# The first eight weight pieces may be scheduled freely, and batch 0's second query part is written ahead of the main loop

## The chip, the cores and the metric

The kernel runs on one core of a Trainium2 chip. The metric is the device time of one execution in microseconds (us); the median of three runs before the change is 893.13 us (891.83 to 895.79). The profile and the trace come from one further, profiled execution. Its engines are called PE (TensorE, matmul), PEld (TensorE's weight loads), DVE (VectorE), ACT (ScalarE), POOL (GpSimd) and SP (SyncE, which issues the DMAs).

## What is computed

Nystrom attention with 32 landmarks on 4 batches of 8 heads (576 positions of 64 values), then two feed-forward networks on its 2304 x 512 output, all in float32:

```python
q_lm, k_lm = means of q and k over 32 blocks of 18 positions
A, Bm, C = softmax(q k_lm'), softmax(q_lm k_lm'), softmax(q_lm k')
Z = Bm' / (norms of Bm)
for _ in range(6):
    Z = 2 * Z - Z @ Bm @ Z
x = A @ Z @ C @ v
x = ((x @ w_a) * (x @ w_b)) @ w_out          # 512 -> 1536 -> 512
h = x @ w_in                                 # 512 -> 2048
out = (h * tanh(softplus(h))) @ w_out2       # 2048 -> 512
```

The weights and the attention inputs come as they are drawn; the weights arrive in 64-bit floating point and are turned into float32 on the core, by bit operations on their two 32-bit words.

## The kernel before

**Attention.** For one batch, `attention` offers its steps by name. kl and ql sum keys and queries over blocks (VectorE, line 136). sB and BB make the small matrix Bm and its setup for the Newton iteration (up to line 182), NS is one Newton step (eight small matmuls, a copy `rz` on ScalarE, an addition on VectorE in line 201; in the sixth the result is spread to the tile zd, line 205). sC0 and sC1 make C's exponentials E (line 213 is the row maximum), ET0 and ET1 transpose them, U multiplies them with v, M gives the 128 x 128 tile `mt`. A0 and A1 are the score products of the first and second half of the queries: a product on TensorE, transposes (line 267), maximum and subtraction on VectorE, the exponential on ScalarE. A0n and A1n end them: sums, division, transposes into `af` (line 283), then the tile `at`, whose high part is copied by ScalarE and whose low part is made by GpSimd (line 286).

**First network.** The product of mt with a group of 512 columns of w_a and w_b gives the tile bm (`emit_bm`), split into a high part (ScalarE) and a low part (VectorE, line 329). A slot (`emit_ab`) multiplies bm with half a batch's `at` in two times six matmuls, multiplies the two results (tg, line 432) and splits the product (g); the output products `ps_o` of w_out follow some slots later. A cell is eight slots: one batch and a third of the columns. The cells go batch 0, batch 1, batch 0, batch 1 and so on, so batch 1's attention has to be done after the first eight slots. In batch 0's first cell the slots alternate by half: slots 0 and 1 take A0's half, slots 2 and 3 A1's.

**Weights.** A group g of w_a and w_b (the tile wab) comes as four pieces of 512 KB. `Units` loads pieces ahead (the first eight into tiles of their own, the later ones into three `stg` tiles), and `step()` converts the next one: `to_f32` takes the absolute value of the high word on ScalarE (Abs), then runs four VectorE instructions (lines 316, 318, 319, 320). When a group is whole it is also written back to DRAM (wabd), to be loaded again for batches 2 and 3. Pieces 0 to 3 are group 0, 4 to 7 group 1; pieces of w_out (tile f, then wo) come behind them.

**What sets the order.** Each engine works through its own queue in order. A scheduler sorts the instructions of each engine when the program is built, by a timing of its own, save that those marked by `tc.keep_in_program_order` stay in written order among themselves on their engine. ScalarE's and TensorE's instructions are marked as long as `Written.on` holds, which is up to the main loop; in `to_f32` Abs and the first VectorE instruction are marked always. The written order of batch 0 is the line of step names (line 552), in which `u` converts a piece and a number is so many filler matmuls on the identity (`fill`). Behind it stand the first bm product, `fill(7)`, A1 and, in the main loop, the rest of the first eight pieces with A1n. A filler of the code is two matmuls in the trace, as are other float32 products of this part.

Of the kernel before, what the change touches and what calls it, by code (L numbers as in the profile page):

```python
# [8 lines left out]
F32 = mybir.dt.float32  # L9
F32R = mybir.dt.float32r  # L10
AF = mybir.ActivationFunctionType
# [20 lines left out]
def nystrom_moe_kernel(ctx: ExitStack, tc: tile.TileContext, q, k, v, w_a, w_b, w_out1, w_in2, w_out2, out):  # L32
# [23 lines left out]
    ac, pe = Written(nc.scalar), Written(nc.tensor)  # L56
# [8 lines left out]
    def bank(tag):  # L65
        return ps.tile([128, 512], F32, tag=tag, bufs=2, name=f"ps_{tag}")
# [33 lines left out]
    def load_v(ap, b):  # L100

        n = H * (D + 1)
        if b:
            t = ap.tile([128, 5, H, D + 1], F32, tag="kv", bufs=1, name="vt")
            nc.sync.dma_start(out=t.rearrange("p i h d -> p (i h d)"), in_=v[b])
            return lambda i: t[:, i]
        ts = []
        for i, w in ((0, 3), (3, 2)):
            t = main.tile([128, 3, H, D + 1], F32, tag="bm", bufs=3, name="vt")
            nc.sync.dma_start(out=t[:, 0:w].rearrange("p i h d -> p (i h d)"), in_=v[b][:, n * i:n * (i + w)])  # L110
            ts.append(t)
        return lambda i: ts[i // 3][:, i % 3]
# [192 lines left out]
        nc.sync.dma_start(out=v, in_=src)  # L305
        return t

    def to_f32(dst, st):
        du = dst.bitcast(U32)
        if len(dst.shape) == 3:  # L310
            st = st.rearrange("p (j f) w -> p j f w", j=dst.shape[1])
            hi, lo = st[:, :, :, 1], st[:, :, :, 0]
        else:
            hi, lo = st[:, :, 1], st[:, :, 0]
        tc.keep_in_program_order(ac.activation(dst, hi.bitcast(F32), AF.Abs))
        i = ve.tensor_scalar(dst, dst, F32_TINY, F32_HUGE, op0=ALU.max, op1=ALU.min)  # L316
        tc.keep_in_program_order(i)
        ve.tensor_scalar(du, du, 3, 0x3FFFFFFF, op0=ALU.logical_shift_left, op1=ALU.bitwise_and)  # L318
        ve.scalar_tensor_tensor(du, hi, 0xC0000000, du, op0=ALU.bitwise_and, op1=ALU.bitwise_or)  # L319
        ve.scalar_tensor_tensor(du, lo, 29, du, op0=ALU.logical_shift_right, op1=ALU.bitwise_or)  # L320
# [32 lines left out]
    def wab_units(g):  # L353
        def conv(i, jj, st):
            if g not in wab:
                wab[g] = main.tile([128, 4, 2, 256], F32, tag="wab", bufs=3, name="wab")
            t = wab[g]
            to_f32(t[:, 2 * jj:2 * jj + 2, i], st)
            if (i, jj) == (1, 1):
                nc.sync.dma_start(out=wabd[g], in_=t.rearrange("p j i f -> p (j i f)"))  # L360

        out = []
        for jj in range(2):
            for i, w in enumerate((w_a, w_b)):
                src = w.bitcast(U32)[256 * jj:256 * jj + 256, 512 * g:512 * g + 512].rearrange("(j p) f -> p j f", p=128)
                out.append((src, 2, lambda st, i=i, jj=jj: conv(i, jj, st)))
        return out
# [5 lines left out]
    def split_unit(dst_hi, dst_lo, st):  # L373
        f = main.tile([128, 512], F32, tag="f24", bufs=2, name="f24")
        if len(dst_hi.shape) == 3:
            f3 = f.rearrange("p (j f) -> p j f", j=dst_hi.shape[1])
        else:
            f3 = f
        to_f32(f, st)
        split(dst_hi, dst_lo, f3, ac, gp if u0.n == 36 else ve)  # L380
# [4 lines left out]
    def wo1_unit(c):  # L385
        def conv(st):
            wo1[c] = main.tile([128, 2, DM], F32R, tag="w", bufs=8, name="wo1")
            split_unit(wo1[c][:, 0], wo1[c][:, 1], st)
            nc.sync.dma_start(out=wo1d[c], in_=wo1[c].bitcast(F32))

        return (w_out1.bitcast(U32)[128 * c:128 * c + 128, :], None, conv)
# [7 lines left out]
    def emit_bm(b, g):  # L399
        p = pair_bank("bm")  # L400
        for c in range(2):
            r = slice(64 * c, 64 * c + 64)
            for j in range(4):
                pe.matmul(
                    p[32 * j:32 * j + 32, c], MT[b][r, 32 * j:32 * j + 32],
                    wab[g][r, j].rearrange("p a f -> p (a f)"), start=True, stop=True,
                )
        t = main.tile([128, 2, 2, 512], F32R, tag="bm", bufs=3, name="bm")
        split(t[:, 0], t[:, 1], p, ac, ve)
        bm[b, g] = t  # L410
# [73 lines left out]
    def to_dram(dst, st):  # L484
        f = main.tile([128, 512], F32, tag="f24", bufs=2, name="f24")
        to_f32(f, st)
        nc.sync.dma_start(out=dst, in_=f if len(dst.shape) == 2 else f.rearrange("p (j f) -> p j f", j=dst.shape[1]))
# [53 lines left out]
    u0 = Units(sum([wab_units(2 * w) + wab_units(2 * w + 1) + [wo1_unit(4 * w + c) for c in range(4)] for w in range(3)], []), early=8)  # L541
    u0.prefetch()
    run0 = attention(ap, 0, kt, qt, load_v(ap, 0))

    def fill(n):

        p = bank("o1")
        for _ in range(n):
            pe.matmul(p[:, 0:128], ident, ident, start=True, stop=True)

    u0.prefetch(10)
    for e in 'kl ql sB sC0 sC1 u 7 BB 8 NS ET0 1 NS ET1 u NS 2 A0 NS u 2 A0n NS U u 3 NS 2 M'.split():
        if e.isdigit():
            fill(int(e))
        elif e == "u":
            u0.step()
        else:
            run0(e)
    emit_bm(0, 0)
    fill(7)  # L560
    run0("A1")
    Written.on = False
    u0.step(4)

    CELLS = [(b + s, w) for b in (0, 2) for w in range(3) for s in range(2)]

# [1 line left out]
    o1q, todo, runs = [], [], {}  # L568
# [1 line left out]
    def load(b):  # L570
        runs[b] = attention(ap, b, *load_qk(ap, b))

    todo = [(1, 0, lambda: run0("A1n"))]
    for b, t0, t1 in ((1, 0.5, 5.5), (2, 27, 41.5), (3, 45, 53.5)):
        todo.append((t0 - (0.4 if b == 1 else 2), 0, lambda b=b: load(b)))
        for n, st in enumerate(STEADY):
# [191 lines left out]
```

## Time and profile before

| | us |
|---|---|
| median of 3 runs (lowest, highest) | 893.13 (891.83, 895.79) |
| the profiled execution's own time | 894.56 |
| its span, first to last instruction | 892.8 |
| TensorE busy | 836.6 (94%) |
| VectorE busy | 426.8 (48%) |
| ScalarE busy | 322.1 (36%) |
| GpSimd busy | 113.6 (13%) |

The shares are means over stages that differ. In the first 100 us the attention of batches 0 and 1, the conversion of the first weights and the first slots run; from then on the first network goes on up to about 470 us, and the second network up to the end. The page's 40 slices of 22.3 us show TensorE at 4, 6, 6 and 8 tenths in the first four and VectorE at 5, 6, 9 and 6.

### The profile page before, as it was taken

The page shows a single profiled execution, that of the slowest core. Times are in us where ns is not written, and L with a number is a line of the kernel's source. Part 1 is how long each engine was busy: PE and PEld are TensorE (multiplying, and loading weights), DVE is VectorE, ACT ScalarE, POOL GpSimd, SP SyncE. Part 2 cuts the span into 40 slices and gives each one's busy share as a digit, 9 for nine tenths or more (in the row PEclk, how much of TensorE's full clock was granted, in tenths as well). Part 3 has the DMA queues.
Part 4 walks back from the last instruction along what each step waited for, and adds up shares of the span by engine and source line. Part 5 has one row for each costly group of instructions (what it writes and reads, how often), then busy time and mean ns, then how long its engine had stood idle before and what let it go on. Part 6 is the DMA issues. An engine that isn't in the chain of part 4 may idle for free.

```text
span 892.8 us, 14633 instructions
## 1 busy us (share of the span) xinstructions
PE 836.6 (94%) x5988; PEld 725.2 (81%) x5988; DVE 426.8 (48%) x828; ACT 322.1 (36%) x668; POOL 113.6 (13%) x131
## 2 busy tenths in 40 slices
PE   4668699999999979999999999999999999999997
PEld 3436387887898947879899999999999999999996
DVE  5696867889366347687796232222112112112111
ACT  3234335534333435444435333323322223232221
POOL 0012212223132124432221000000000000000000
PEclk9668599999999979999999999999999999999999
DMA  9432654659542313546777321201101101000000
GB/s 359 167 113 99 244 166 165 197 186 320 208 158 90 122 52 119 185 154 205 244 242 228 98 71 48 60 1 60 48 0 31 41 1 47 26 1 8 28 1 36
DMA packets 38387, 103.26 MB, mean 116 GB/s; under 512 B 3120, under 2 KB 11312, under 8 KB 35376
## 3 DMA queue, kind: packets, MB, share of 16 engines
q1 hardware_dynamic: 38320, 102.33, 33.6%
q8 instruction: 47, 0.77, 0.4%
q14 instruction: 20, 0.16, 0.1%
HBM read 74.01 MB, written 28.31 MB: 115 GB/s over the span
## 4 chain that ended last, share of the span: by engine, by line
PE 79%; DVE 11%; DMA 3%; ACT 3%; issue 3%; POOL 1%; ACTq 0%; SPq 0%; DVEq 0%
PE ps_ab L49 36%; PE ps_o L49 21%; PE ps_bm L49 12%; PE ps_at L49 9%; DVE f L319 1%; DMA wi2d<-f 1%; DVE f L316 1%; DVE tg L432 1%; ACT f L49 1%; DMA xs<-x2d 1%; DVE f L320 1%; DVE f L318 1%; DMA kt<-in_k_dram 1%; DVE kl L136 1%; DVE stA L277 0%
## 5 line engine op out<-in xcount | busy, mean ns | idle before, releaser
L49 PE MATMUL ps_ab<-xhl,wi 128*128 128x384 f32 x1152 | 219.8, 338 | 0.0
L49 PEld LDWEIGHTS ps_ab<-xhl,wi 128*128 128x128 f32 x1152 | 205.4, 188 | 8.1
L49 PE MATMUL ps_ab<-at,bm 128*128 128x288 f32 x1152 | 190.2, 305 | 6.9 <-ACT bm L49 2.0
L329 DVE TENSOR_TENSOR g<-m,g 128x384 fp32r<-128x384 f32 x96 | 53.5, 558 | 299.3 <-ACT g L49 299.3
L49 PEld LDWEIGHTS ps_ab<-at,bm 128*128 128x128 f32 x1152 | 164.1, 192 | 38.6 <-issue 13.4
L49 PE MATMUL ps_o<-g,wo 128*128 128x288 f32 x1152 | 183.1, 300 | 9.5 <-ACT wo L49 4.7
L49 PEld LDWEIGHTS ps_o<-g,wo 128*128 128x128 f32 x1152 | 162.8, 190 | 23.6 <-issue 5.8
L49 ACT ACTIVATE m<-ps_ab 128x384 f32<-128x384 f32 x96 | 47.1, 492 | 264.7 <-PE ps_ab L49 264.6
L329 POOL TENSOR_TENSOR g<-tg,g 128x288 fp32r<-128x288 f32 x96 | 85.3, 890 | 289.7 <-ACT g L49 287.5
L49 PE MATMUL ps_bm<-wo,g 128*128 128x512 f32 x288 | 81.6, 392 | 0.0
L49 PE MATMUL ps_at<-wo,g 128*128 128x512 f32 x288 | 75.1, 393 | 0.0
L49 PE MATMUL ps_o<-wo,g 128*128 128x512 f32 x288 | 74.5, 393 | 0.0
L49 ACT ACTIVATE g<-tg 128x288 fp32r<-128x288 f32 x96 | 42.5, 443 | 87.3 <-DVE tg L432 87.2
L49 PEld LDWEIGHTS ps_bm<-wo,g 128*128 128x128 f32 x288 | 54.1, 188 | 12.4
L432 DVE TENSOR_TENSOR tg<-ps_ab,ta 128x288 f32<-128x288 f32 x96 | 43.3, 451 | 38.9 <-PE ps_ab L49 28.7
L49 PEld LDWEIGHTS ps_o<-wo,g 128*128 128x128 f32 x288 | 53.6, 188 | 8.6
L49 PEld LDWEIGHTS ps_at<-wo,g 128*128 128x128 f32 x288 | 53.5, 188 | 8.2
L49 ACT ACTIVATE ta<-ps_ab 128x288 f32<-128x288 f32 x96 | 38.9, 405 | 53.6 <-PE ps_ab L49 53.0
L49 ACT ACTIVATE g<-m 128x384 fp32r<-128x384 f32 x96 | 50.3, 524 | 4.4 <-PE ps_o L49 1.4
L49 PE MATMUL ps_bm<-wab,mt 64*32 64x512 f32 x384 | 46.3, 686 | 1.1 <-ACT mt L49 1.1
L329 DVE TENSOR_TENSOR bm<-ps_bm,bm 128x1024 fp32r<-128x1024 f32 x24 | 29.3, 1219 | 24.7 <-ACT bm L49 24.6
L320 DVE SCALAR_TENSOR_TENSOR f<-stg,f 128x512 uint32<-128x512 uint32 x44 | 36.7, 833 | 0.6
(122 smaller groups left out, 603.1 us busy)
## 6 DMA issues: line engine op xcount, KB each, us to landing
stg<-in_moe_w_out_dram SPq DMA_DIRECT2D x28, 512.0 KB, 3.8
stg<-in_moe_w_in_dram SPq DMA_DIRECT2D x16, 512.0 KB, 4.7
stg<-in_moe_w_a_dram SPq DMA_DIRECT2D x12, 512.0 KB, 5.3
stg<-in_moe_w_b_dram SPq DMA_DIRECT2D x12, 512.0 KB, 5.8
wabd<-wab SPq DMA_DIRECT2D x6, 1024.0 KB, 4.8
wo1d<-wo SPq DMA_DIRECT2D x12, 512.0 KB, 4.5
wab<-wabd SPq DMA_DIRECT2D x6, 1024.0 KB, 5.4
wo<-wo1d SPq DMA_DIRECT2D x12, 512.0 KB, 5.6
```

The costliest lines, as they stand in the source:

```text
L49: i = f(*a, **kw)
L136: i = ve.tensor_reduce(out=x[nm][:, j:j + 2], in_=src[:, j:j + 2].rearrange("p j (t k) -> p j t k", k=BLK), axis=AX, op=ALU.add,)
L316: i = ve.tensor_scalar(dst, dst, F32_TINY, F32_HUGE, op0=ALU.max, op1=ALU.min)
L318: ve.tensor_scalar(du, du, 3, 0x3FFFFFFF, op0=ALU.logical_shift_left, op1=ALU.bitwise_and)
L319: ve.scalar_tensor_tensor(du, hi, 0xC0000000, du, op0=ALU.bitwise_and, op1=ALU.bitwise_or)
L320: ve.scalar_tensor_tensor(du, lo, 29, du, op0=ALU.logical_shift_right, op1=ALU.bitwise_or)
L329: lo_eng.tensor_tensor(dst_lo, src, dst_hi.bitcast(F32), op=ALU.subtract)
L432: ve.tensor_tensor(tg, pb[:, 0:288], ta, op=ALU.mult)
```

## The change

Four edits. `to_f32` gets an argument `held`; with `held=False` neither Abs nor the first VectorE instruction is marked, so the scheduler may place them where it likes. Pieces of groups 0 and 1 are converted so. A fifth `u` stands at the end of the list of steps. The seven fillers behind the first bm product are replaced by one piece, and A1n is written directly behind A1, ahead of the main loop, no longer as its first task; two pieces follow it in place of four. The same eight pieces are converted, by the same instructions.

```diff
-    def to_f32(dst, st):
+    def to_f32(dst, st, held=True):
...
-        tc.keep_in_program_order(ac.activation(dst, hi.bitcast(F32), AF.Abs))
+        i = ac.engine.activation(dst, hi.bitcast(F32), AF.Abs)
+        if held:
+            tc.keep_in_program_order(i)
         i = ve.tensor_scalar(dst, dst, F32_TINY, F32_HUGE, op0=ALU.max, op1=ALU.min)
-        tc.keep_in_program_order(i)
+        if held:
+            tc.keep_in_program_order(i)
...
-            to_f32(t[:, 2 * jj:2 * jj + 2, i], st)
+            to_f32(t[:, 2 * jj:2 * jj + 2, i], st, g > 1)
...
-    for e in 'kl ql sB sC0 sC1 u 7 BB 8 NS ET0 1 NS ET1 u NS 2 A0 NS u 2 A0n NS U u 3 NS 2 M'.split():
+    for e in 'kl ql sB sC0 sC1 u 7 BB 8 NS ET0 1 NS ET1 u NS 2 A0 NS u 2 A0n NS U u 3 NS 2 M u'.split():
...
     emit_bm(0, 0)
-    fill(7)
+    u0.step()
     run0("A1")
     Written.on = False
-    u0.step(4)
+    run0("A1n")
+    u0.step(2)
...
-    todo = [(1, 0, lambda: run0("A1n"))]
+    todo = []
```

What the scheduler makes of it is seen in the order of the instructions. ScalarE's queue from its start, before (`wab<-stg` is a piece's Abs, `eb` and `E` the exponentials of sB and sC, `rz` the copy of a Newton step, `ET` that of a transpose):

```order
L49 ACT_TABLE_LOAD x3
L49 ACTIVATE eb<-eb 128x64
L49 ACTIVATE E<-ps_at,stC 128x288 x2
L49 ACTIVATE E<-ps_bm,stC 128x288 x2
L49 ACTIVATE wab<-stg 128x2x256
L49 ACTIVATE rz<-ps_bm 128x2x32
L49 ACTIVATE ET<-ps_at 128x512
```

The same place after the change:

```order
L315 ACTIVATE wab<-stg 128x2x256 x2
L49 ACTIVATE eb<-eb 128x64
L315 ACTIVATE wab<-stg 128x2x256
L49 ACTIVATE E<-ps_at,stC 128x288 x2
L49 ACTIVATE E<-ps_bm,stC 128x288 x2
L315 ACTIVATE wab<-stg 128x2x256 x5
L49 ACTIVATE rz<-ps_bm 128x2x32
L49 ACTIVATE ET<-ps_at 128x512
```

All eight Abs now stand ahead of the first copy of a Newton step, where one stood.

VectorE's queue behind the first two slots, before (`stB`, `eb`, `bc` are small softmax steps of batch 1, `stC` its row maxima, `sa` and `af` the second query part of batch 0; line 319 and 320 are the last two instructions of a piece):

```order
L319 SCALAR_TENSOR_TENSOR wab<-stg,wab 128x2x256
L280 TENSOR_TENSOR sa<-sa,stA 128x576
L153 TENSOR_TENSOR eb<-ps_at,stB 128x64
L320 SCALAR_TENSOR_TENSOR wab<-stg,wab 128x2x256
L316 TENSOR_SCALAR wab<-wab 128x2x256
L213 TENSOR_REDUCE stC<-ps_bm 128x2
L283 STREAM_TRANSPOSE af<-sa 128x288 x2
L155 TENSOR_REDUCE stB<-eb 128x2
L318 TENSOR_SCALAR wab<-wab 128x2x256
L213 TENSOR_REDUCE stC<-ps_at 128x2
```

The same place after the change:

```order
L280 TENSOR_TENSOR sa<-sa,stA 128x576
L153 TENSOR_TENSOR eb<-ps_at,stB 128x64
L283 STREAM_TRANSPOSE af<-sa 128x288 x2
L213 TENSOR_REDUCE stC<-ps_bm 128x2
L155 TENSOR_REDUCE stB<-eb 128x2
L156 TENSOR_SCALAR stB<-stB 128x2
L157 RECIPROCAL stB<-stB 128x2
L159 TENSOR_TENSOR bc<-eb,stB 128x2x32
L161 STREAM_TRANSPOSE bc<-bc 128x32 x2
L213 TENSOR_REDUCE stC<-ps_at 128x2
```

The piece instructions are gone from here (they now stand ahead of the first query part's transposes), and one row maximum stands behind the transposes of `af`.

TensorE's queue at the first bm product (`ps_bm<-wab,mt`), before (`ps_o` from `ident` alone is a filler, `ps_at<-qt,kl` the product of A1, `ps_ab` the first two slots):

```order
L49 MATMUL ps_bm<-zd,U 64x128 x2
L49 MATMUL ps_bm<-wab,mt 32x512 x8
L49 MATMUL ps_o_476<-ident 128x128 x7
L49 MATMUL ps_at<-qt,kl 32x288 x8
L49 MATMUL ps_ab<-at,bm 128x288 x24
```

The same place after the change:

```order
L49 MATMUL ps_bm<-zd,U 64x128 x2
L49 MATMUL ps_bm<-wab,mt 32x512 x8
L49 MATMUL ps_at<-qt,kl 32x288 x8
L49 MATMUL ps_ab<-at,bm 128x288 x24
```

The seven fillers are gone, and the product of A1 follows the bm product at once.

## Rows read from the trace of the kernel before

**Rows 1.** Windows: stretch, length, busy us (PE, PEld, DVE, ACT, POOL), clock, DMA, GB/s

```profile
44.00:46.00 2.00, 2.00 (x25) 1.41 (x25) 0.55 (x2) 0.00 (x0) 0.00 (x0) 0.85 0.00 0
50.00:52.00 2.00, 0.00 (x0) 0.00 (x0) 2.00 (x3) 1.69 (x4) 0.53 (x1) 0.85 0.03 9
70.00:72.00 2.00, 2.00 (x12) 1.25 (x17) 0.83 (x4) 0.41 (x1) 0.00 (x0) 0.53 0.95 393
...
98.00:104.00 6.00, 3.43 (x52) 2.29 (x42) 5.95 (x16) 1.47 (x3) 0.00 (x0) 0.50 0.78 287
...
140.00:180.00 40.00, 40.00 (x302) 33.97 (x301) 34.13 (x59) 21.49 (x45) 9.11 (x10) 1.00 0.62 205
...
480.00:893.00 413.00, 407.81 (x2052) 370.14 (x2052) 84.29 (x153) 127.21 (x252) 1.71 (x2) 1.00 0.12 39
```

**Rows 2.** Timeline of SP's DMA issues: start us, length us, queue, line, what

```profile
12.26 1.07 SPq L305 DMA_DIRECT2D stg<-in_moe_w_b_dram  x1
```

**Rows 3.** DMA issues from 12.2 to 12.6: last number is us to landing

```profile
stg<-in_moe_w_b_dram SPq DMA_DIRECT2D x1, 512.0 KB, 12.0
```

**Rows 4.** Timeline, 0 to 46: start, length, engine, line, what [idle before <-releaser]

```profile
8.84 2.61 DVE L136 TENSOR_REDUCE ql<-qt 128x64 f32<-128x1152 f32 x2 [0.20 <-DMA qt<-in_q_dram]
...
16.95 0.69 ACT L49 ACTIVATE wab<-stg 128x512 f32<-128x512 f32 x1
...
20.91 0.22 ACT L49 ACTIVATE rz<-ps_bm 128x64 f32<-128x64 f32 x1 [3.28 <-PE ps_bm L49]
...
24.89 0.21 DVE L201 TENSOR_TENSOR rz<-ps_bm,rz 128x64 f32<-128x64 f32 x1
...
34.74 1.41 POOL L286 TENSOR_TENSOR at<-af,at 128x576 fp32r<-128x576 f32 x1 [32.74 <-ACT rz L49]
...
39.91 1.96 PE L49 MATMUL ps_bm<-wab,mt 64*32 64x512 f32 x16 [0.37 <-ACT mt L49]
41.80 3.15 PE L49 MATMUL ps_o<-ident 128*128 128x128 f32 x14
...
45.70 0.85 DVE L267 STREAM_TRANSPOSE sa<-ps_at 128x288 f32<-128x288 f32 x2 [1.45 <-PE ps_at L49]
```

**Rows 5.** Timeline, 46 to 82, same columns

```profile
51.60 0.95 DVE L316 TENSOR_SCALAR wab<-wab 128x512 f32<-128x512 f32 x1
...
56.02 1.30 DVE L319 SCALAR_TENSOR_TENSOR wab<-stg,wab 128x512 uint32<-128x512 uint32 x1
...
59.65 0.82 DVE L283 STREAM_TRANSPOSE af<-sa 128x288 f32<-128x288 f32 x2
...
61.27 1.40 POOL L286 TENSOR_TENSOR at<-af,at 128x576 fp32r<-128x576 f32 x1 [4.49 <-ACT at L49]
...
68.14 3.25 PE L49 MATMUL ps_ab<-at,bm 128*128 128x288 f32 x12
...
70.16 0.22 DVE L181 TENSOR_TENSOR rz<-ist,rz 128x64 f32<-128x64 f32 x1
...
74.95 0.21 DVE L201 TENSOR_TENSOR rz<-ps_at,rz 128x64 f32<-128x64 f32 x1
...
79.98 1.85 PE L49 MATMUL ps_ab<-at,bm 128*128 128x288 f32 x12
```

**Rows 6.** Groups of VectorE's instructions up to 107 us: count | busy us, mean ns

```profile
L319 DVE SCALAR_TENSOR_TENSOR wab<-stg,wab 128x512 uint32<-128x512 uint32 x8 | 6.0, 747 | 0.1
L320 DVE SCALAR_TENSOR_TENSOR wab<-stg,wab 128x512 uint32<-128x512 uint32 x8 | 5.8, 730 | 0.0
...
L316 DVE TENSOR_SCALAR wab<-wab 128x512 f32<-128x512 f32 x8 | 4.4, 554 | 2.1 <-ACT wab L49 2.1
...
L318 DVE TENSOR_SCALAR wab<-wab 128x512 uint32<-128x512 uint32 x8 | 3.3, 417 | 0.0
```

**Rows 7.** Timeline, 100 to 112, same columns

```profile
106.80 0.28 ACT L49 ACTIVATE mt<-ps_at 128x128 f32<-128x128 f32 x1 [2.27 <-PE ps_at L49]
```

## The prediction

> **What bounds the kernel now.** I read the windows by stage first [rows 1]. From 140 us on TensorE is busy all the time (40.00 of 40 us in 140 to 180, 407.81 of 413 us in 480 to 893), at a granted clock of 1.00, so nothing there can be gained by moving VectorE work; a microsecond won or lost earlier is simply carried to the end. Before about 107 us it is otherwise: in 50 to 52 TensorE does nothing and VectorE works 2.00 of 2 us, in 98 to 104 VectorE works 5.95 of 6 and TensorE 3.43. There the end is set by two chains that share VectorE: the attention of batch 0 (it ends in the first bm product at 39.91 [rows 4]) and that of batch 1 (it ends in mt at 106.80 [rows 7]), behind which the steady stretch begins. So the whole question is: at what time does the new kernel reach the step that stands at 106.80?
>
> **What the change moves.** Eight weight pieces are converted early on, numbered 0 to 7 here (four of group 0, four of group 1). Each is one Abs on ScalarE, 0.69 us [rows 4], and four VectorE instructions, on the mean 0.55 + 0.42 + 0.75 + 0.73 = 2.45 us [rows 6]; that mean holds two or three that ran slow (0.95 and 1.30 [rows 5]), and an undisturbed piece is about 2.2 us, or 1.9 where other instructions stand between its own and start some 0.08 us before the one ahead has ended. Before, pieces 0 to 3 stand among the steps of batch 0 and pieces 4 to 7 behind the first slots, up to 69 us. Now all eight stand ahead of the third Newton step of batch 0, and nothing of them is left behind it. I went through the new order engine by engine, from the end of the ql sums at 8.84 + 2.61 = 11.45 us [rows 4], with the durations of the rows.
>
> Step 1, the cost on ScalarE. A piece can't be converted before it has landed. The last, piece 7, is issued at 12.26 and takes 12.0 us, so it is there at 24.3 [rows 2, 3]. The issue times don't hang on the conversions, so they stay. ScalarE works in order, and its new order puts the Abs of pieces 3 to 7 ahead of the copy of the first Newton result. That copy ran at 20.91 [rows 4]; now it can't run before 24.3 + 0.7 = 25.0. Floor of the loss at this place: 4.1 us.
>
> Step 2, the cost on VectorE. All eight pieces, 8 x 1.9 = 15.2 us (8 x 2.45 = 19.6 at most), and the small softmax steps stand between 11.45 and the third Newton addition. Row by row the last piece instruction ends at 31 to 32 us, so that addition, at 24.89 before [rows 4], comes 6 to 7 us late.
>
> Step 3, what comes back within batch 0. Before, the rest of piece 1 and pieces 2 and 3 stood between that addition and zd, some 6 us of VectorE, of which about half lay beside waits for ScalarE and TensorE. That is gone, so 6 to 7 late shrinks to 3.0 late at the first bm product: it ends at 44.9, not at 39.91 + 1.96 = 41.87 [rows 4].
>
> Step 4, the filler. Behind that product TensorE ran 14 filler matmuls, 3.15 us, ahead of the second score product A1 [rows 4]. They are removed, and A1 now follows at once. VectorE's transposes of A1 stand behind the low part of bm (the high part on ScalarE and the low part on VectorE come to some 2.3 us after the product), so they start at 47.2, not at 45.70 [rows 4]: 1.5 late.
>
> Step 5, the first gain. Between these transposes and those at the end of the second query part (59.65 [rows 5]) five piece instructions stood: 0.95 and 1.30 as shown [rows 5], and 0.42 + 0.73 + 0.42 by [rows 6], less the overlaps: 3.4 us. One row maximum (0.7) that stood ahead of the transposes now stands behind. 1.5 - 3.4 - 0.7: 2.6 early, I take 2.4. GpSimd's low part, 61.27 + 1.40 [rows 5], then ends at 60.3, and TensorE can start the slots of the second half then.
>
> Step 6, the second gain. From 59.65 to the end of the setup of batch 1's Newton chain (70.16 [rows 5]) eleven piece instructions stood, about 6.3 us by [rows 6]. Not all is won, for the setup needs a product that TensorE makes only behind the slot that starts at 60.3, at the low clock. I get 65.3 to 67.1: 3 to 4.9 early. The second bm product no longer waits for piece 7 and is out of the way before batch 1's first Newton product; that one stands behind a slot of 12 matmuls at the low clock (3.25 us [rows 5]), and its addition, at 74.95 before [rows 5], comes at 70.1 to 70.8: 4.2 to 4.9 early.
>
> Step 7, the rest. From there to mt the order differs in a few places that stand a row or two apart, and behind mt it is the same on all engines. The chain in between is made of the same waits; carried through, mt comes 4.2 to 5.3 us early. I take 4.8. The copies of groups 0 and 1 back to DRAM are issued earlier, in the time when the input loads run; the next key tile may land 2 us later than before, and it is needed only at about 50. That costs nothing; if it did slip past 50, each microsecond would count.
>
> Sum: +3.0 at the first bm product, -1.5 for the filler, -3.9 by step 5 and about -2.4 more by steps 6 and 7: -4.8 us. The profiled execution took 894.56 us (its span 892.8 us and 1.76 around it), so 889.8 in its terms; it lies 1.43 above the median of the runs, 893.13, and on that scale the forecast is 888.3.
>
> **Rivals.**
> First, half the gain: "same". It decides on what a piece costs when it is mixed with others. If each costs 2.2 and not 1.9 us in steps 1 and 2, the eight end 2.4 us later, everything behind comes later by that, and 4.8 shrinks to 2.4: 890.7. For it speaks that all the forms that ran slow in the trace (0.95, 1.30 [rows 5]) did so beside GpSimd work, against it that GpSimd stands idle up to 34.74 [rows 4]. TensorE at the low clock from 60 to 72, which doesn't shrink with VectorE's load, holds the gain down to the same 2.4 us of step 5.
>
> Second, more: the clock rises earlier. The granted clock rose from 0.50 to 1.00 within 44 to 46 (mean 0.85), fell again within 50 to 52 (0.85) and was only just rising in 70 to 72 (0.53) [rows 1]. In the new order TensorE works in a row from 60.3 on. If it is at 2.4 GHz already by 66, a slot of 12 matmuls takes 1.85 and not 3.25 us [rows 5], two of these and the bm product give some 3 us more: -7.8, 885.3.
>
> Third, slower: the clock stays low. The filler that goes is 3.15 us of TensorE work that stood directly ahead of the place where the clock rose, and in its place there are now two pauses of 0.5 to 1.2 us; the first stretch of slots may then run at 1.2 GHz. There it costs nothing, VectorE is behind it. But if the clock is still low from 72 to 89, the four slots and the output products there, at 1.4 us more for a slot [rows 5], cost 5.6 for the slots and up to 3 more for the rest: 8.3 against a gain of 4.8, +3.5, 896.6. It turns slower where the clock has not risen by about 82. Against it: past 60.3 TensorE has work in a row for more than 20 us, as it had from 62.7 to the rise past 70.
> The Trainium skill, "TensorE: Matmul & The Clock Gate" (Part 1: The HAM clock gate), calls the throttled state the default, from which only activity releases. By that rule alone, filler removed ahead of a rise is a loss; the trace shows the rise behind the filler, but also that VectorE, not TensorE, ends the stretch that follows it.
>
> **How the numbers follow.** Forecast (3.3 to 6.3 us won) 0.50, half the gain 0.27, more 0.16, slower 0.07. About 0.5%, 4.5 us, is what a measurement of this kernel can tell from no change. The forecast straddles it: 0.32 of its 0.50 lies above. So faster 0.32 + 0.16 = 0.48; same 0.18 + 0.27 = 0.45; slower 0.07. The range goes from the better part of the second rival (8.3 won) to 1 us won, where half the gain is nearly lost to the spread of the runs: 884.8 to 892.2.
>
> **What would show it.** In the new profile: the copy of the first Newton result at 25 to 26 and the third addition at 31 to 32 (steps 1, 2); the first bm product ending at 44.5 to 46 (step 3); transposes of A1 at 47 to 48 (step 4); those of the second query part at 57 to 58 (step 5); batch 1's first Newton addition at 70 to 71 (step 6); mt at 101.5 to 102.6 (step 7); and TensorE at 40.00 of 40 from there on. I am wrong if the third addition comes past 34 (a piece costs more than 2.2), if the clock is low anywhere between 75 and 85, or if mt is early and the span isn't shorter by the same.

## Result and profile after

The changed kernel takes 885.55 us (median of 7 runs, 883.71 to 888.62) against 895.26 us for the kernel before (median of 7 runs beside it, 891.83 to 896.39). The ratio is 0.991, with a 95% interval of 0.9893 to 0.9926: 0.7 to 1.1% faster (the two medians alone give 0.989). The forecast was 888.3 us in a range of 884.8 to 892.2. Its sign was right; its size was not. The forecast had 4.8 us to win; the spans of the two profiled executions differ by 892.8 - 884.3 = 8.5 us. The time is that of the second rival (885.3). The forecast was counted from the first median of before, 893.13; counted from the median beside it, 895.26, the whole range would stand 2.1 us higher and the time below it. So the gain is at the far end of the range, not in its middle.

The first line of the page of the kernel after:

```profile
span 884.3 us, 14605 instructions
```

The timeline of after (start us, length us, engine, line, operation, what). These are the rows that answer to [rows 4, 5, 7]; added lines shift the numbers by two to four, so that a piece's four VectorE instructions are lines 318, 321, 322 and 323, and the Abs is line 315:

```profile
23.53 0.67 ACT L315 ACTIVATE wab<-stg 128x512 f32<-128x512 f32 x1 [0.62 <-DMA stg<-in_moe_w_b_dram]
23.85 0.22 DVE L181 TENSOR_TENSOR rz<-ist,rz 128x64 f32<-128x64 f32 x1
...
24.69 0.23 ACT L49 ACTIVATE rz<-ps_bm 128x64 f32<-128x64 f32 x1 [0.49 <-PE ps_bm L49]
...
28.93 1.28 DVE L323 SCALAR_TENSOR_TENSOR wab<-stg,wab 128x512 uint32<-128x512 uint32 x2
...
30.14 0.22 DVE L201 TENSOR_TENSOR rz<-ps_bm,rz 128x64 f32<-128x64 f32 x1
...
42.03 1.09 PE L49 MATMUL ps_bm<-wab,mt 64*32 64x512 f32 x16 [0.37 <-ACT mt L49]
...
45.43 0.84 DVE L267 STREAM_TRANSPOSE sa<-ps_at 128x288 f32<-128x288 f32 x2
...
55.57 0.84 DVE L283 STREAM_TRANSPOSE af<-sa 128x288 f32<-128x288 f32 x2
...
57.20 1.44 POOL L286 TENSOR_TENSOR at<-af,at 128x576 fp32r<-128x576 f32 x1 [1.07 <-ACT at L49]
57.21 1.45 DVE L156 TENSOR_SCALAR stB<-stB 128x2 f32<-128x2 f32 x1
...
58.69 2.77 PE L49 MATMUL ps_ab<-at,bm 128*128 128x288 f32 x10 [0.66 <-POOL at L286]
...
62.36 1.67 PE L49 MATMUL ps_bm<-wab,mt 64*32 64x512 f32 x16
63.96 1.85 PE L49 MATMUL ps_ab<-at,bm 128*128 128x288 f32 x12
...
66.72 0.22 DVE L201 TENSOR_TENSOR rz<-ps_at,rz 128x64 f32<-128x64 f32 x1
...
97.66 0.28 ACT L49 ACTIVATE mt<-ps_at 128x128 f32<-128x128 f32 x1 [2.27 <-PE ps_at L49]
```

The last piece instruction of the first two groups ends at 30.2, where before one ended at 69. Piece 7's Abs still waits for its transfer (23.53), but it does not hold the copy of the first Newton result: ScalarE is through with it at 24.20, and the copy starts at 24.69, when the product ahead of it is done (its row names PE as what it waited for). That product starts at 24.21, 0.36 us behind the start of the setup's last step on VectorE (line 181, 23.85), as in before (20.07 and 20.43); the profile puts its wait down to the Abs, which ends at the same time. The step in the timeline of before:

```profile
20.07 0.22 DVE L181 TENSOR_TENSOR rz<-ist,rz 128x64 f32<-128x64 f32 x1
```

The third Newton addition is 5.3 us later than before and mt 9.1 us earlier. Behind mt the gain is carried on: the last of the four batches' mt stands at 326.6 before and 318.0 after.

The windows of after (stretch, length, busy us of PE, PEld, DVE, ACT, POOL, granted clock, DMA share, GB/s), to be read beside [rows 1]:

```profile
40.00:42.00 2.00, 1.47 (x25) 1.02 (x24) 0.72 (x3) 0.28 (x1) 0.00 (x0) 1.00 0.00 0
...
62.00:64.00 2.00, 2.00 (x41) 0.56 (x33) 1.24 (x6) 1.04 (x3) 0.36 (x1) 0.60 0.03 8
...
82.00:84.00 2.00, 0.00 (x0) 0.00 (x0) 0.86 (x3) 1.22 (x3) 0.00 (x0) 0.50 0.31 125
```

The granted clock is 1.00 (2.4 GHz) already in 40 to 42, where before it rose within 44 to 46, and again from about 63.6, where before 70 to 72 still reads 0.53. In 82 to 84 it is low again.

To say where the forecast and the trace part, I cut the way at four rows and take the differences between neighbours (forecast: the middle of what the prediction gives):

| stretch | before | forecast | after |
|---|---|---|---|
| start to A1's transposes (L267) | 45.70 | 47.2 | 45.43 |
| from there to the second part's (L283) | 13.95 | 10.0 | 10.14 |
| from there to batch 1's first Newton addition (L201) | 15.30 | 13.25 | 11.15 |
| from there to mt | 31.85 | 31.55 | 30.94 |
| sum: mt | 106.80 | 102.0 | 97.66 |

The second stretch came out as forecast. The first was won by 1.8 us more, the third by 2.1, the fourth by 0.6. Two theories for these 4.5 us: **V**, VectorE alone (the pieces cost less early and held up more late than I had it), and **C**, TensorE's clock (it rose sooner in both places). The experiments take the change apart and then go for the clock.

### The profile page after: what moved, and what is told of

It reads as the page before. It is cut to its first block, busy times and chain, and to the rows that moved or that the text cites. A ratio compares the mean times of both kernels' runs of the same rounds, so it can differ in the third digit from the quotient of the medians.

```text
span 884.3 us, 14605 instructions
## 1 busy us (share of the span) xinstructions
PE 831.8 (94%) x5974; PEld 724.4 (82%) x5974; DVE 427.5 (48%) x828; ACT 323.3 (37%) x668; POOL 113.3 (13%) x131
## 4 chain that ended last, share of the span: by engine, by line
PE 83%; DVE 9%; DMA 3%; ACT 2%; issue 1%; POOL 1%; ACTq 0%; SPq 0%; DVEq 0%
PE ps_ab L49 38%; PE ps_o L49 22%; PE ps_bm L49 13%; PE ps_at L49 10%; DMA xs<-x2d 1%; DMA qt<-in_q_dram 1%; DVE f L323 1%; DVE f L322 1%; DVE f L318 1%; DMA wo<-wo1d 1%; DVE ql L136 1%; DVE tg L435 1%; DVE wab L322 1%; ACT f L315 1%; DVE stA L277 0%
## 5 line engine op out<-in xcount | busy, mean ns | idle before, releaser
L49 PEld LDWEIGHTS ps_ab<-at,bm 128*128 128x128 f32 x1152 | 163.8, 192 | 35.0 <-issue 13.4
L49 ACT ACTIVATE m<-ps_ab 128x384 f32<-128x384 f32 x96 | 47.2, 492 | 264.2 <-PE ps_ab L49 264.2
L435 DVE TENSOR_TENSOR tg<-ps_ab,ta 128x288 f32<-128x288 f32 x96 | 43.4, 452 | 41.4 <-PE ps_ab L49 29.0
L49 PE MATMUL ps_bm<-wab,mt 64*32 64x512 f32 x384 | 43.8, 671 | 1.1 <-ACT mt L49 1.1
```

The costliest lines, as they stand in the source:

```text
L49: i = f(*a, **kw)
L435: ve.tensor_tensor(tg, pb[:, 0:288], ta, op=ALU.mult)
```

## Experiments

Every kernel computes the whole reference; the fillers that some add or drop are matmuls whose result nobody reads. Ratios are against the kernel before on the same chip.

**Which part of the change pays.** First the change with the filler back in its place; the pieces are free, and the weight step and A1n stand where the change puts them.

```diff
     emit_bm(0, 0)
+    fill(7)
     u0.step()
```

> After, with the seven filler matmuls put back ahead of A1: on every engine's list this is the kernel before with nothing but the eight pieces freed. Theory V (VectorE: the gain comes from the pieces leaving the stretch 48 to 69, the filler only decides when A1 starts): A1's first transposes go from 45.43 in after to 47 to 48.6, the af copy of the second part (L283, 55.57 in after) waits for VectorE's row maxima and stays within 0.5 or goes to at most 57, and the last-but-three column, the first mt, lies at 97.7 to 99; time 885.5 to 887. Theory C (TensorE's clock: about 3.5 us of the 8.5 come from its being at 1.00 from 40 and from 64 on): the filler is more work at the front, so the clock still rises at 40, and the row of the first bm product still reads about 1.09 us; what happens after 52 can go either way, mt 97 to 99. If removing the filler were the change's main part, mt would be at 104 or later and the time 892 or more.

Measured 887.46 us, ratio 0.9936 (0.9916 to 0.9955). Its timeline:

```profile
41.85 1.83 PE L49 MATMUL ps_o<-ident 128*128 128x128 f32 x14
...
55.47 0.83 DVE L283 STREAM_TRANSPOSE af<-sa 128x288 f32<-128x288 f32 x2
...
97.60 0.28 ACT L49 ACTIVATE mt<-ps_at 128x128 f32<-128x128 f32 x1 [1.39 <-PE ps_at L49]
```

The filler runs at the high clock, 1.83 us and not 3.15, and mt stands where it stands in after. So the larger part of the gain comes without the filler's removal, which with free pieces gives nothing that this profile shows. The times leave more open: the interval overlaps that of after (0.9893 to 0.9926) by 0.001, and between the two ratios lie 2.3 us. The profiled execution, at 885.77 us, is one of the faster of this kernel.

Then the text moves without the freeing:

```diff
-            to_f32(t[:, 2 * jj:2 * jj + 2, i], st, g > 1)
+            to_f32(t[:, 2 * jj:2 * jj + 2, i], st)
```

> After, with all eight pieces held in written order again: the filler is gone and the query part stands ahead of the main loop, but VectorE has the late pieces between batch 1's steps. Theory V: the 11 piece instructions are back ahead of batch 1's Newton setup; setup end L181 at 69 to 70.5, first Newton addition of batch 1 at 73.5 to 75, mt 105.3 to 106.8 (before: 106.80), time 893 to 895. Theory C says the same of the pieces and says in addition that the clock follows the density of TensorE's work: first bm product at 1.96 (low), the twelve-matmul slot near 68 at 3.25. If the text moves alone carried the gain, mt would be 98 to 101 and the time 886 to 889.

Measured 890.07 us, ratio 0.9961 (0.9947 to 0.9975). Both theories had expected almost nothing, and both missed. Its timeline:

```profile
40.78 0.43 DVE L318 TENSOR_SCALAR wab<-wab 128x512 f32<-128x512 f32 x1 [1.65 <-ACT wab L315]
...
56.23 0.84 DVE L283 STREAM_TRANSPOSE af<-sa 128x288 f32<-128x288 f32 x2
...
101.62 0.28 ACT L49 ACTIVATE mt<-ps_at 128x128 f32<-128x128 f32 x1 [0.47 <-PE ps_at L49]
```

I had overlooked that one weight step now stands ahead of the bm product and one directly behind it. Though held, pieces 4 and 5 thus run at 40.8 to 48.5, the first of them in the 4.2 us in which VectorE of before waits for the bm copy, and not behind 51.6. That wait in the timeline of before:

```profile
43.03 1.22 DVE L329 TENSOR_TENSOR bm<-ps_bm,bm 128x1024 fp32r<-128x1024 f32 x1 [4.23 <-ACT bm L49]
```

Half of the late pieces are out of the way without any freedom, and mt comes 5.2 us earlier. To part this from the filler, before without the filler and nothing else:

```diff
-    fill(7)
```

> Before, without the seven filler matmuls of 41.80 (3.15 us) ahead of A1 and with nothing else changed; all pieces stay held and late, pieces 4 to 7 between 51 and 69. With the text moves alone mt came 5.2 earlier, and this tells the filler's part of that from that of the weight step which stands one product earlier there (pieces 4 and 5 at 40.8 to 48.4, where VectorE had 4.2 us of nothing). Theory V: A1's transposes 1 to 1.6 earlier, 44.1 to 44.8, the second part's af copy 58 to 59 for 59.65, as its row sums stand behind the pieces, mt 105.3 to 106.5, time 891.5 to 894. If the filler were the larger part: mt 102 to 103.5, time 889.5 to 891.

Measured 891.22 us, ratio 0.997 (0.9943 to 0.9998). Its timeline:

```profile
44.15 0.84 DVE L267 STREAM_TRANSPOSE sa<-ps_at 128x288 f32<-128x288 f32 x2
...
58.06 0.82 DVE L283 STREAM_TRANSPOSE af<-sa 128x288 f32<-128x288 f32 x2
...
65.75 1.87 PE L49 MATMUL ps_ab<-at,bm 128*128 128x288 f32 x12
...
71.71 0.21 DVE L201 TENSOR_TENSOR rz<-ps_at,rz 128x64 f32<-128x64 f32 x1
...
104.66 0.28 ACT L49 ACTIVATE mt<-ps_at 128x128 f32<-128x128 f32 x1 [2.28 <-PE ps_at L49]
```

With the pieces late, the filler costs 1.6 us at A1 and at the second part, as step 4 had it, and mt 2.1 (the first Newton addition 3.2; the clock then fell again, from 71.7 to 75). The other 3.0 of the text moves' 5.2 come with the weight step and A1n, which stand earlier; that it is the weight step is argued from the rows above, no run parts the two. At mt the gains don't add: text moves 5.2, freeing with the filler in place 9.2, all together 9.1. These are single executions, and two of one kernel differ by 1.6 us there, as shown below. The times can't confirm it: text moves 0.39% and freeing with the filler 0.64% come to 1.03%, and the whole change has 0.7 to 1.1%.

Last, only the second group free, the first held as before:

```diff
-            to_f32(t[:, 2 * jj:2 * jj + 2, i], st, g > 1)
+            to_f32(t[:, 2 * jj:2 * jj + 2, i], st, g != 1)
```

> After, with only the pieces 4 to 7 (the second group) free, and the pieces 0 to 3 held in written order. Theory V: the gain is that of the pieces 4 to 7, which alone stood between 47 and 69; batch 1's setup end L181 at 64 to 65.5 and mt at 97 to 98.5, time 884.5 to 887; the price at the start (the third Newton addition at 30.14 instead of 24.89) stays within 1.5 of after's since piece 7 lands at 23.5 in any order. Were the freeing of the first group what pays, mt would be at 101 or later, as with the text moves alone (101.6).

Measured 890.33 us, ratio 0.9959 (0.9945 to 0.9973), mt at 102.18: V missed here. VectorE's timeline:

```profile
40.73 0.68 DVE L323 SCALAR_TENSOR_TENSOR wab<-stg,wab 128x512 uint32<-128x512 uint32 x1
...
47.18 0.83 DVE L267 STREAM_TRANSPOSE sa<-ps_at 128x288 f32<-128x288 f32 x2
...
56.59 1.40 DVE L280 TENSOR_TENSOR sa<-sa,stA 128x576 f32<-128x576 f32 x1
57.91 0.74 DVE L213 TENSOR_REDUCE stC<-ps_bm 128x2 f32<-128x576 f32 x1
...
58.71 0.82 DVE L283 STREAM_TRANSPOSE af<-sa 128x288 f32<-128x288 f32 x2
```

No piece stands in 47 to 69 any more, yet half the gain is missing. Pieces stand among batch 0's steps up to 41.4, the first bm product runs at the low clock (42.92, 1.96 us), and A1's transposes come 1.75 later than in after; then L280 takes 1.40 us instead of 0.76, and a row maximum stands ahead of L283 again. It may count, then, that all eight pieces are done by 30, and not only that the late four are gone. But the low clock at the first bm product is a rival that this run does not exclude: 0.9 of the 1.75 us are that product's, and two runs below, with all eight pieces done by 31 and that product slow too, have mt at 101.45 and 100.45.

**The clock at the first bm product.** After without any of the fillers in batch 0's steps, then without only the last two groups of them:

```diff
-    ... u 7 BB 8 NS ET0 1 NS ET1 u NS 2 A0 NS u 2 A0n NS U u 3 NS 2 M u
+    ... u BB NS ET0 NS ET1 u NS A0 NS u A0n NS U u NS M u
```

> After, without the fillers between the query part's steps (7, 8, 1, 1, 2, 2, 3 and 2 matmuls; the results do not use them). Theory V: fillers are off the path; TensorE has less to do, so the steps end at the same time or up to 0.5 us earlier; mt 97.2 to 97.9, time 885 to 886.5. Theory C: the fillers of 38.56 and 40.22 keep the clock at 1.00 for the first bm product; without them it runs at the low clock, 1.96 instead of 1.09 for that product, the four M matmuls and the A1 transposes likewise, so A1's transposes start at 46 to 47.5 and mt is 1 to 3 us later, 98.7 to 100.7, time 886.5 to 889.

Measured 888.83 us, ratio 0.9952 (0.9936 to 0.9969). The timeline:

```profile
43.67 1.96 PE L49 MATMUL ps_bm<-wab,mt 64*32 64x512 f32 x16 [0.37 <-ACT mt L49]
...
47.93 0.84 DVE L267 STREAM_TRANSPOSE sa<-ps_at 128x288 f32<-128x288 f32 x2
...
69.54 0.23 DVE L201 TENSOR_TENSOR rz<-ps_at,rz 128x64 f32<-128x64 f32 x1
...
101.45 0.28 ACT L49 ACTIVATE mt<-ps_at 128x128 f32<-128x128 f32 x1 [2.27 <-PE ps_at L49]
```

mt is 3.8 us later than in after, where C says 1 to 3 and V nothing; 2.5 of it are there at A1. But part of that is from the start: here the last step of batch 0's setup stood at 26.95, not at 23.85 as in after, because the scheduler had also put VectorE's rows in another order. So only the last two groups:

```diff
-    ... U u 3 NS 2 M u
+    ... U u NS M u
```

> After, without the fillers of 3 and 2 matmuls that stand between the last Newton steps and M (all other fillers stay; the run without any filler also lost the clock at 20 to 30 and ran its first Newton steps late, so it does not tell the two apart). Theory V (VectorE's pieces alone): nothing waits for these five matmuls; third Newton addition 30.1, second part's af copy 55.6, mt 97.4 to 98.0, time 885 to 886.5. Theory C (the clock): the granted clock at 40 to 44 falls to 0.50, the first bm product reads 1.96 instead of 1.09, the A1 transposes start at 46.3 to 47 instead of 45.43, and mt comes 0.8 to 1.6 later, 98.5 to 99.3, time 886.4 to 888.

Measured 887.35 us, ratio 0.9919 (0.9897 to 0.9941). The first bm product still reads 1.09 us (at 40.23), A1's transposes 43.63, mt 96.55: C's price was wrong here, for the clock was up at 38 without these fillers.

**The clock at 60 to 72.** The same twelve fillers in batch 1's last score step, once in before and once in after:

```diff
-            eb = sm([128, 2, LM], "eb")
+            eb = x["eb"] = sm([128, 2, LM], "eb")
...
+            if b == 1 and r:
+                f = bank("o1")
+                for _ in range(4):
+                    pe.matmul(f[:, 0:128], ident, x["ql"].rearrange("p j l -> p (j l)"), start=True, stop=True)
...
+            if b == 1 and r:
+                for _ in range(8):
+                    pe.matmul(f[:, 0:64], ident, x["eb"].rearrange("p c l -> p (c l)"), start=True, stop=True)
```

> Before, all pieces held, with 12 filler matmuls more in batch 1's last score step: four on the query sums (ahead of its scores), eight of 64 columns on the softmax row behind it, where TensorE stands idle at 56.4 to 58.3 and 59.5 to 62.7. Theory V: VectorE's pieces set the path; L181 stays at 70.2 to 71.5 and the first Newton addition of batch 1 follows it by 4.8 as in [before: 70.16 and 74.95]; mt 106.8 to 108.3, time 893 to 896. Theory C: the clock is at 1.00 from 62 to 64 on instead of 72; the twelve-matmul slot reads 1.85 instead of 3.25, the second bm product about 1.1 instead of 1.92, and the way from L181 to the first Newton addition shrinks from 4.8 to 2.3 to 3.2 (after: 2.28; text moves alone: 3.15), so mt comes 1 to 2.5 earlier than before's, 104.3 to 105.8, time 891 to 893.5: this is then the part of the gain that is the clock's and not the pieces'.

Measured 894.2 us, ratio 0.9994 (0.9978 to 1.0011): no change. A row of the timeline and then two windows of before with fillers:

```profile
63.40 1.59 PE L49 MATMUL ps_ab<-at,bm 128*128 128x288 f32 x10 [0.65 <-POOL at L293]
```

```profile
60.00:62.00 2.00, 2.00 (x30) 1.56 (x15) 2.00 (x7) 0.69 (x1) 0.09 (x1) 1.00 0.31 55
...
66.00:68.00 2.00, 0.51 (x24) 0.51 (x28) 1.97 (x7) 1.45 (x4) 0.00 (x0) 0.71 0.00 0
```

The clock was at 1.00 from 60 on and the slot of ten took 1.59 us, but VectorE was full in these windows with its pieces (2.00 and 1.97 of 2 us), TensorE soon stood idle (0.51 of 2 us in 66 to 68), and the clock fell back. mt came at 106.27. Here a clock that was raised while VectorE was late bought nothing.

> After, with the same 12 fillers in batch 1's last score step, so that TensorE's hole between the scores and the second half of the slot is filled. Theory C: the clock is back at 1.00 by 58 to 60 instead of 63.3, the ten-matmul slot of 58.69 reads 1.5 to 2 instead of 2.77, the second bm product 1.09 instead of 1.67; mt 95.7 to 97, time 883.5 to 885.5. Theory V: fillers ahead of the scores make batch 1's row maximum 0.5 to 1.8 later and VectorE has nothing to do meanwhile; mt 98 to 99.5, time 886 to 888.

Measured 885.94 us, ratio 0.9901 (0.9877 to 0.9926), no different from after. The timeline of after with fillers, and a window:

```profile
60.13 1.83 PE L49 MATMUL ps_ab<-at,bm 128*128 128x288 f32 x12
...
66.13 0.21 DVE L201 TENSOR_TENSOR rz<-ps_at,rz 128x64 f32<-128x64 f32 x1
...
97.69 0.28 ACT L49 ACTIVATE mt<-ps_at 128x128 f32<-128x128 f32 x1 [2.27 <-PE ps_at L49]
```

```profile
58.00:60.00 2.00, 2.00 (x21) 1.80 (x16) 1.24 (x4) 0.37 (x1) 0.50 (x1) 0.88 0.42 78
```

The clock is up from 58.5 on, five microseconds before after's, the first Newton addition comes 0.6 earlier, and at mt nothing is left of it. Other fillers, on batch 1's key sums:

```diff
-                if first and nm == "ql":
+                if b < 2 and nm == "ql":
```

> After, with six filler matmuls of 128 columns on batch 1's key sums, put ahead of its two query sums: they fill TensorE's hole at 49.3 to 52.8 (3.47 us), from which the granted clock falls to 0.50 at 54 to 62 in after. Theory V: VectorE's row maxima and POOL's row of 57.20 set the path there; the fillers cost nothing or 0.3 us; mt 97.6 to 98.2, time 885.5 to 886.5. Theory C: the clock stays at 1.00 through 54 to 64, the ten-matmul slot (2.77 us at 58.69) takes about 1.5, the second bm product (1.67) 1.09, and mt comes 1 to 2.5 us earlier, 95.2 to 96.7, time 883 to 885. Where the fillers are too few or too early to keep the clock, the window 54:62 still reads 0.50 and nothing moves; that would leave C open.

Measured 888.31 us, ratio 0.9942 (0.9922 to 0.9963), mt at 99.89. Both theories missed: V wanted 97.6 to 98.2, C 95.2 to 96.7. The fillers kept the clock at 1.00 up to 57 instead of 53, but it then fell for 57 to 64, under the very slots that C wanted faster. That tells nothing for C's prices.

**Is the clock the schedule's, or chance?** Both kernels once more:

> The kernel before once more, for a second profiled execution. If the clock is a property of the schedule, the first bm product reads 1.96 again and the granted clock comes back to 1.00 at 70 to 72; mt 106.3 to 107.3. If it is chance from one execution to the next, the product can read 1.09 and the rise can lie anywhere from 60 to 72, with mt 103 to 107.

> The kernel after once more. If the clock is a property of the schedule: first bm product 1.09, clock back at 1.00 at 62 to 64, mt 97 to 98.5. If it is chance: the product may read 1.96 and mt lie at 98.5 to 101.

Before took 895.42 us (span 893.6), after 881.37 (span 879.6). A window of before's second execution, its mt, then the timeline of after's:

```profile
72.00:74.00 2.00, 1.59 (x28) 0.26 (x16) 0.34 (x1) 1.10 (x2) 0.79 (x1) 0.82 0.48 197
```

```profile
107.36 0.28 ACT L49 ACTIVATE mt<-ps_at 128x128 f32<-128x128 f32 x1 [2.28 <-PE ps_at L49]
```

```profile
40.65 1.09 PE L49 MATMUL ps_bm<-wab,mt 64*32 64x512 f32 x16 [0.37 <-ACT mt L49]
...
54.19 0.84 DVE L283 STREAM_TRANSPOSE af<-sa 128x288 f32<-128x288 f32 x2
...
96.04 0.28 ACT L49 ACTIVATE mt<-ps_at 128x128 f32<-128x128 f32 x1 [2.27 <-PE ps_at L49]
```

Before's pattern repeats, with its first bm product at 1.96 us and its late rise, at 72.7 after 71.9. After's repeats in kind, but by mt the two executions of one program are 1.6 us apart. 1.2 of them arise between the third Newton addition and A0's transposes (30.14 to 31.52 in the first, where VectorE waits 1.17 us for TensorE, and 30.03 to 30.19 in the second). The clock was not the same in the two there: 0.50 in 28 to 32 in the first, 1.00 in the second.

The last run frees the pieces of all six groups:

```diff
-            to_f32(t[:, 2 * jj:2 * jj + 2, i], st, g > 1)
+            to_f32(t[:, 2 * jj:2 * jj + 2, i], st, False)
```

> After, with the pieces of all six groups free (groups 2 to 5 run between 98 and some 500 us, where TensorE is busy at 1.00 most of the time). Theory V: their VectorE work is beside TensorE's, nothing waits for it and nothing is gained: 884.5 to 887.5, mt of the first batches within 0.5 of after's. A rival: freed pieces go ahead of what TensorE's next product waits for (the sums of ps_ab, the row maxima of batches 2 and 3), as the freed first groups did at the start, where the third Newton addition came 5.2 later; 888 to 893.

Measured 888.05 us, ratio 0.9934 (0.9908 to 0.996); the interval overlaps that of after, so neither expectation is settled. It answers another question. Up to 83 us its order is that of after, and this execution happened to have the low clock in all of 34 to 44. Its timeline:

```profile
42.76 1.74 PE L49 MATMUL ps_bm<-wab,mt 64*32 64x512 f32 x16 [0.40 <-ACT mt L49]
...
46.83 0.84 DVE L267 STREAM_TRANSPOSE sa<-ps_at 128x288 f32<-128x288 f32 x2
...
56.97 0.84 DVE L283 STREAM_TRANSPOSE af<-sa 128x288 f32<-128x288 f32 x2
...
65.81 0.21 DVE L181 TENSOR_TENSOR rz<-ist,rz 128x64 f32<-128x64 f32 x1
```

At the low clock the front comes out as I had forecast it: 46.83 for 47.2, 56.97 for 57.2, 65.81 for 65.3 to 67.1. In part that is luck: the third Newton addition stood at 30.00, 1.5 us ahead of the forecast, and the way from there to the end of the first bm product took 14.5 us for a forecast 13.4. mt was at 100.45.

## Why the prediction was right in sign and short in size

- **The bound** held in the main: what is won ahead of mt reaches the end. In the first pair, 9.1 at mt became 8.5 in the span. In single executions the two differ by more: after without fillers won 5.4 at mt and 3.5 in the span, after with the twelve fillers 9.1 and 12.8.
- **Step 1** had the copy's time about right (24.69 for 25 to 26) but not what sets it. ScalarE was free at 24.20; the copy waited for VectorE's setup, by way of the product. In six other executions with free pieces, piece 7 landed later than in this one and the copy did run right behind its Abs, at 24.8 to 25.0, and the third addition still came at 30.0 to 30.2. So ScalarE's floor cost nothing.
- **Step 2** was right in mechanism, 1 to 2 us dear: third addition at 30.14 (31 to 32), pieces done by 30.2. From 11.4 to there VectorE is never idle, and from start to next start the piece instructions take 15.2 of these 18.7 us, the 8 x 1.9 of the prediction.
- **Step 3** was the first mis-sized term: 3.0 late at the end of the first bm product was 43.12 - 41.87 = 1.25. Of the 1.8 us, 0.9 is the product itself, 1.09 instead of the 1.96 that I carried over from [rows 4]; the rest came with step 2, whose addition was 1.4 sooner, less 0.5 by which the way from there to the product was longer than forecast. With the clock low at that place the forecast rows came out within 0.4 us (the run with all groups free), in part by the luck told there. I had treated the clock of [rows 1] as fixed there.
- **Step 4** was right where it doesn't count: the filler costs 1.6 us at A1 with the pieces late, but in the freed kernel it runs at the high clock, and putting it back moved neither the second part's transposes nor mt in the execution profiled.
- **Step 5** was right: 10.14 us from A1's transposes to the second part's, forecast 10.0.
- **Step 6** was the second mis-sized term: 11.15 us to the first Newton addition, forecast 13.25. Its words were that this product "stands behind a slot of 12 matmuls at the low clock (3.25 us [rows 5])". That slot took 1.85 us, and the second bm product 1.67 instead of 1.92: 1.65 of the 2.1 us. The run without the filler shows the same with the pieces left where they were: 13.65 instead of 15.30, its slot 1.87.
- **Step 7** carried the gain through and was 0.6 us short; I didn't follow where that arose.
- **The second rival** named part of what was wrong (clock up by 66, the slot 1.85). That its time, 885.3, was nearly exact is luck in part: it had all of its 3 us behind 60.3, where the rows give 2.1, and the other 1.8 was won ahead of A1, where it saw nothing. I gave it 0.16 because [rows 1] showed one late rise. That was weak: of fourteen profiled executions only the two of before had the clock up as late as 72; the others had it up between 58 and 68. The rival's reason, TensorE working in a row past 60.3, isn't enough here: so it did in before from 62.7.
- But more clock is not more gain. Once the pieces are gone, a rise at 58.5 (fillers in after) or at 67 (no fillers at all) changes the way from L283 to the first Newton addition only from 10.7 to 11.5 us, and with the pieces in the way the raised clock fell again. The freeing is the larger lever; by the rows the clock gave some 2.5 us on top in the first pair (0.9 in step 3, 1.65 in step 6). That it rises sooner because of the freeing is not shown. It does go with mt: with all eight pieces free, the six executions whose first bm product took 1.09 us have mt at 96.0 to 99.9, the two with a slower one at 100.45 and 101.45.
- **The first rival** is out: a piece cost 1.9 us of VectorE, not 2.2.
- **The third rival** is out: the clock was up from 63.6 to 80.7. In the two runs without the filler and with held pieces it rose at 64.7 and 64.6, and not at 72 as in before's two. The Trainium skill, "TensorE: Matmul & The Clock Gate" (Part 1: The HAM clock gate), was cited for activity as what releases the throttle; by that alone, taking work out ahead of a rise should not bring it forward. In these two executions the rise came sooner without it.
- **One sign** that I had set for being wrong came true: the clock is low between 75 and 85, at 0.50 from 82 on. It refutes nothing, for the slots that the third rival priced were over at 75.3 (in before at 84.0). I should have tied the sign to these slots, not to a time.

Open: what sets the rise in before at 72 in both executions. TensorE is busy without a gap from 62.7 there, and in the run without the filler, whose rows in that stretch are the same and 1.6 us earlier, it rose some 7 us sooner. Nor do the runs part the clock in the first 40 us, which differs between executions of one program, from the schedule: the first bm product read 1.09 in six executions with free pieces and fillers, 1.74 in a seventh, and 1.96 in all six that held some pieces and in the one without fillers.

No version tried beats after by more than the intervals: after with fillers is at 0.9901 and after with two fillers less at 0.9919, where after has 0.991.

## What to carry to other kernels

Work that only has to be done sometime should be allowed to run where its engine waits, and it pays most when that takes it out of a later stretch in which the same engine sets the pace; moving half of it one product earlier by hand (the text moves alone) gave about half of the gain at mt. When a sum is made from rows at the low clock, make it a second time with the rows at the high clock wherever TensorE's work moves closer together, and give that sum a chance of its own. Don't add gains measured one at a time without a look at the trace: at mt, 5.2 and 9.2 came to 9.1 here.

## What was not expected of the hardware

The same program with the same data does not get the same clock. Beside the first 40 us, single dips come and go in the steady part. The windows of after's two executions, the first and then the second:

```profile
200.00:240.00 40.00, 38.22 (x365) 32.68 (x365) 22.59 (x51) 16.93 (x37) 10.23 (x11) 0.96 0.67 244
```

```profile
200.00:240.00 40.00, 38.22 (x389) 32.48 (x388) 23.29 (x51) 17.36 (x39) 9.90 (x11) 1.00 0.68 240
```

TensorE's busy time there is 38.22 us in both, the clock 0.96 and 1.00, and the trace has 365 and 389 matmuls in it; another such dip stands in 400 to 440 of the first alone. The spans are 884.3 and 879.6 us, of which 1.6 us were there at mt. The Trainium skill, "TensorE: Matmul & The Clock Gate" (Part 1: The HAM clock gate), says that the number of slow matmuls at a kernel's start varies from run to run of one kernel. No run here shows that at the start, where the clock reads 1.00 up to 16 us in all fourteen executions; they show a like variation later on. A difference of 4.7 us is about the spread of the runs of one kernel (883.71 to 888.62 us), and it is why kernels whose mt differs by a microsecond can't be told apart here by their times.

VectorE's small instruction of line 156 took 1.45 us in after while GpSimd made the low part (57.20, 1.44 us), for 0.16 at its first time there (16.40); in the run with only the second group free it took 0.12, and line 280 met an instruction of GpSimd instead (56.58, 0.80 us) and took 1.40 for 0.76. Which instruction pays goes by what stands beside GpSimd's.
